# Attention on one Trainium2 core: the 256-column parts of two neighbouring heads share a PSUM bank, one exponential and the last step of the row maximum

## The chip, the cores and the metric

The kernel runs on one core of one Trainium2 chip. The time is device microseconds of that core for one execution of the whole program; lower is better. Instructions are issued to five queues: TensorE (PE: matmuls, and PEld for the weight loads ahead of them), VectorE (DVE), ScalarE (ACT), GpSimd (POOL) and SyncE (SP: DMAs). PSUM has eight banks of 128 x 512 fp32; a tile of scores takes one bank.

## The reference, cut to what matters

Two independent halves are computed and put side by side: attention with a memory that is carried over four segments (`A`), and a two-dimensional spectral filter (`B`, FFT, product, inverse FFT). The change touches the softmax of `A` alone. There are 32 heads of width 18, and each of the 4 segments has 512 rows.

```python
for s in range(N):                      # N = 4 segments of L = 512 rows
    qs, ks, vs = q[:, :, s], k[:, :, s], v[:, :, s]
    logits = jnp.einsum("bhqd,bhkd->bhqk", qs, ks) * scale + mask   # causal
    p = _softmax(logits, axis=-1)
    a_dot = jnp.einsum("bhqk,bhkd->bhqd", p, vs)
    ...                                 # a_mem from M and z, then the gate
    o = g * a_mem + (1.0 - g) * a_dot
outs @ wo
```

## The kernel before, in words

The program has three stages. The FFT and the projections of q, k and v come first, the inverse FFT follows with the first attention steps woven into it, and from about 348 us on there is attention alone, with the output projection and the work on the memory as background. The edits lie in attention.

**Steps and groups.** There are 128 pairs of a head and a segment. The loop in `attention` (L986) has one step `t` for each, and four steps make a group `k` (`k, hh = divmod(t, 4)`; 32 groups). Each step runs two passes over different heads, because the maximum of a row must be known before its exponentials:

- `s1` (L679) makes the scores of pair `t+11`, rows on partitions, to find each row's maximum. The 512 x 512 scores are causal, so the four row blocks have 128, 256, 384 and 512 columns. They go into banks of the pool `ps1` (tag `s1`, three banks) as three tiles, which I call **A** (384 and 128 columns in one bank), **B** (512) and **C** (256). For each block DVE adds the mask and takes the maximum in one instruction (L690), whose result lands in `mg`; the reduced products themselves go to a scratch tile `junk`.
- `mpath` (L698) turns a group's 16 columns of maxima into rows: POOL splits them into two bf16 parts `mh` (L702, L703), PE transposes them into `mt` (L706, which also takes a bank of tag `s1`), ACT copies that to `mts` (L709), and a DMA puts it under `Q` as two more contraction rows. It begins at the end of an even step (`hh==0`) and its transpose stands in the odd step after that (`hh==1`).
- `s2` (L714) makes the scores of pair `t` again, transposed and with the maximum subtracted by those two rows, in three tiles of the pool `ps` (tag `s2`, three banks), **P0** (512 columns, L722), **P1** (384 and 128, L726 and L727) and **P2** (256, L731). ACT turns each into exponentials (L723, L728, L732) in the SBUF tiles `P[0]`, `P[1]`, `P[2]` of the group. When a group's fourth head is done, POOL zeroes what lies above the diagonal (L736, `affine_select`), two tiles at once and two (`rest`) one step later.
- `pv` (L745) is the product with v: in the steps with `t%4==1` and `t%4==3`, a burst of 16 matmul records for the whole group before.

Steps with `hh` 0 or 2 are called even here and have no burst; those with `hh` 1 or 3 are odd and have one. Within a step the order is written out by hand in `attention`: A, P0, B, P1, then the burst in odd steps, then one piece of background (`run_bg`), then C, the transpose where there is one, and P2. PE runs them in this order, and a scheduler does not move them. A tile of `s1` takes the bank of a tile that DVE has finished reading, most often the third one back, so A of a step waits for A of the step before, and so on; where the transpose has taken a bank, the tiles behind it move up by one.

Background that matters below: `combine` (L853), `mem1` (L826) and `oproj` (L891) issue matmuls into the single bank of tag `post`, and DVE multiplies what they make (L836, L881, L883: `am` or `ux` times `pb`). `recip` (L772) puts a reciprocal of 128 x 128 on DVE (L780). From `t=117` on there is no `s1` any more (the tail).

Of the kernel before, what the change touches and what calls it, by code (L numbers as in the profile page):

```python
# [5 lines left out]
F32=mybir.dt.float32; F32R=mybir.dt.float32r  # L6
AF=mybir.ActivationFunctionType; OP=mybir.AluOpType
# [358 lines left out]
BF=mybir.dt.bfloat16  # L366
# [43 lines left out]
class ATT:  # L410
# [268 lines left out]
    def s1(s,t):  # L679

        nc=s.nc; k,hh=divmod(t,4); n,qd=divmod(k,2); h=4*qd+hh
        Q,K=s.Qs[n%3],s.Ks[n%4]; tp=s.sm
        assert (n,0) in s.loaded and (n,1) in s.loaded,(t,n)
        if hh==0: s.mg[k]=tp.tile([128,4,4],F32,name="mg")
        def part(*J):
            p=s.ps1.tile([128,512],F32,name="s1",tag="s1")
            for o,i in J: nc.tensor.matmul(p[:,o:o+128*i+128],Q[:108,h,128*i:128*i+128],K[:108,h,:128*(i+1)],start=True,stop=True)  # L687
            for o,i in J:
                w=128*(i+1); b=256*(1+i//2); junk=tp.tile([128,b],BF,name=f"junk{b}",bufs=1)
                nc.vector.tensor_tensor_reduce(out=junk[:,:w],in0=p[:,o:o+w],in1=s.mask[:,512-w:],scale=1.0,scalar=-3.0e38,  # L690
                    op0=OP.add,op1=OP.max,accum_out=s.mg[k][:,hh,i:i+1])
        part((0,2),(384,0))
        yield
        part((0,3))
        yield
        part((0,1))
        yield
    def mpath(s,k):  # L698

# [14 lines left out]
    def s2(s,t):  # L714
        nc=s.nc; k,hh=divmod(t,4); n,qd=divmod(k,2); h=4*qd+hh
        Q,K=s.Qs[n%3],s.Ks[n%4]; tp=s.tp
        if hh==0: s.P[k]=[tp.tile([128,4,w],F32,name=f"P{i}") for i,w in enumerate((512,512,256))]
        P=s.P[k]
        q=lambda o: Q[:110,h,o:]
        kk=lambda j: K[:110,h,128*j:128*j+128]  # L720
        p0=s.ps.tile([128,512],F32,name="s2",tag="s2")
        nc.tensor.matmul(p0,kk(0),q(0),start=True,stop=True)  # L722
        nc.scalar.activation(P[0][:,hh],p0,AF.Exp,scale=SC)  # L723
        yield
        p1=s.ps.tile([128,512],F32,name="s2",tag="s2")
        nc.tensor.matmul(p1[:,:384],kk(1),q(128),start=True,stop=True)  # L726
        nc.tensor.matmul(p1[:,384:],kk(3),q(384),start=True,stop=True)  # L727
        nc.scalar.activation(P[1][:,hh],p1,AF.Exp,scale=SC)  # L728
        yield
        p2=s.ps.tile([128,256],F32,name="s2",tag="s2")  # L730
        nc.tensor.matmul(p2,kk(2),q(256),start=True,stop=True)  # L731
        nc.scalar.activation(P[2][:,hh],p2,AF.Exp,scale=SC)  # L732
        r=slice(0,4) if k<31 else (slice(0,3) if hh==2 else slice(3,4))
        if hh==3 or k==31 and hh==2:
            def sel(x):
                nc.gpsimd.affine_select(out=x[:,r],in_=x[:,r],pattern=[[0,r.stop-r.start],[1,128]],compare_op=OP.is_ge,fill=0.0,base=0,channel_multiplier=-1)  # L736
            sel(P[0][:,:,:128])
            sel(P[1][:,:,384:])
            def rest():
                sel(P[1][:,:,:128])  # L740
                sel(P[2][:,:,:128])
            if k<31: s.rest=rest
            else: rest()
        yield
    def pv(s,k,jj):  # L745

# [437 lines left out]
```

## Time and profile before

| what | value |
|---|---|
| time, median of 3 executions | 689.67 us (688.49 to 689.87) |
| time of the profiled execution | 689.55 us |
| its span, first to last instruction | 687.8 us |
| PE busy | 671.8 us (98%) |
| DVE busy | 543.0 us (79%) |
| ACT busy | 440.4 us (64%) |
| POOL busy | 192.1 us (28%) |
| granted TensorE clock | 1.00 throughout |
| stretch 618 to 650 us (the tail) | PE busy 29.05 of 32.00 us, DVE 22.85, ACT 22.09 |

Times are from one profiled execution. The 1.75 us between its own time and its span lie outside what the profile shows. The busy time of PE counts each matmul to its modelled end, and such ends overlap the next matmul, so a PE that reads as busy may still be waiting for a bank; waits show as longer distances between the starts of matmuls. In the same way two DVE instructions in a row overlap by some 0.07 us, so a duration is longer than the distance from one start to the next. Rows of the timeline read: start, duration, engine, line, operation, output<-input, size, count, and in square brackets the idle time before and what ended it.

### The profile page before, as it was taken

Reading aid. Unit: us, or ns where it says so; the run is one execution under the profiler, and the core shown is the slowest. Engines: PE = TensorE matmul, PEld = TensorE weight load, DVE = VectorE, ACT = ScalarE, POOL = GpSimd, SP = SyncE. Lnnn points to the kernel's source line nnn. Section 1 sums busy time; section 2 is a strip of 40 time slices with the busy share of each in tenths; the row PEclk is TensorE's granted clock in tenths of the full one; section 3 lists DMA queues with packets and bytes.
Section 4 is the critical chain, followed back from the end, with each engine's and each line's share of the span. In section 5 each row is a group of like instructions: output and inputs, shape, how many; then the busy total and the mean of one; then the engine's idle time right before and its main releaser. Section 6 shows DMA issues by size and latency. Waiting matters only on the chain.

```text
span 687.8 us, 14313 instructions
## 1 busy us (share of the span) xinstructions
PE 671.8 (98%) x4776; PEld 486.7 (71%) x4776; DVE 543.0 (79%) x1509; ACT 440.4 (64%) x964; POOL 192.1 (28%) x389
## 2 busy tenths in 40 slices
PE   9999999999999999999989999999999999998997
PEld 5999779879879879899954444444566445663497
DVE  5998989889789679598678888988856988567643
ACT  3876795675685474544468877777766777666531
POOL 2111000100200102566325533435323563235310
PEclk9999999999999999999999999999999999999999
DMA  9896466595486679799337775765656567423152
GB/s 338 297 307 185 144 190 196 168 302 178 136 235 209 198 207 306 195 282 272 100 107 193 198 185 161 208 191 155 171 154 185 152 171 165 125 80 97 29 166 80
DMA packets 76035, 127.58 MB, mean 185 GB/s; under 512 B 12812, under 2 KB 44202, under 8 KB 72370
## 3 DMA queue, kind: packets, MB, share of 16 engines
q1 hardware_dynamic: 69310, 110.67, 55.7%
q0 software_dynamic: 5632, 15.76, 8.1%
q8 instruction: 37, 0.61, 0.4%
q10 hardware_dynamic: 1020, 0.25, 0.2%
q14 instruction: 36, 0.29, 0.2%
HBM read 81.78 MB, written 43.92 MB: 183 GB/s over the span
## 4 chain that ended last, share of the span: by engine, by line
PE 84%; DVE 5%; ACT 3%; DMA 3%; issue 3%; POOL 1%; SPq 0%; ACTq 0%; DVEq 0%; POOLq 0%
PE pj L487 15%; PE pv L754 11%; PE s L687 11%; PE pjv L487 7%; PE po L902 7%; PE i L331 4%; PE i L320 4%; PE f L145 4%; PE c L166 4%; PE s L722 3%; PE s L726 3%; PE po L931 2%; PE pn L829 2%; DVE junk L690 2%; PE pm L559 2%
## 5 line engine op out<-in xcount | busy, mean ns | idle before, releaser
L690 DVE CUSTOM_DVE_ANT_0 junk<-s,x 128x384 bf16<-128x384 f32 (+3 forms) x512 | 222.7, 487 | 48.1 <-PE s L687 47.2
L736 POOL TENSOR_SCALAR_AFFINE_SELECT P<-P 128x512 f32<-128x512 f32 (+2 forms) x132 | 79.2, 625 | 75.4 <-ACT P L723 73.7
L754 PE MATMUL pv<-P,vs 128*32 128x512 f32 (+3 forms) x1024 | 82.2, 439 | 0.2 <-POOL P L736 0.2
L723 ACT ACTIVATE P<-s 128x512 f32<-128x512 f32 x128 | 77.6, 606 | 6.3 <-PE s L687 2.1
L728 ACT ACTIVATE P<-s 128x512 f32<-128x512 f32 x128 | 77.7, 607 | 3.4 <-PE s L727 3.1
L732 ACT ACTIVATE P<-s 128x256 f32<-128x256 f32 x128 | 49.7, 389 | 45.0 <-PE s L731 44.8
L687 PE MATMUL s<-Ks,Qs 108*128 108x384 bf16 (+3 forms) x256 | 65.2, 300 | 3.0 <-DVE mg L690 2.3
L754 PEld LDWEIGHTS pv<-P,vs 128*32 128x32 f32 x1024 | 26.8, 109 | 45.2 <-issue 34.8
L487 PE MATMUL pj<-x,wqkh 128*128 128x512 f32 x162 | 56.1, 408 | 0.0
L232 DVE TENSOR_TENSOR Z<-Z 128x580 f32<-128x580 f32 (+2 forms) x51 | 45.9, 913 | 0.6
L687 PEld LDWEIGHTS <-Qs 108*128 108x128 bf16 x320 | 31.2, 98 | 19.2 <-issue 12.4
L690 DVE DVE_READ_ACCUMULATOR2_ANT mg<- 128x1 f32 x512 | 42.5, 83 | 0.0
L548 POOL MEMSET vt<- 128x32 f32 x16 | 2.4, 162 | 139.5 <-PE pm L559 125.5
L320 PE MATMUL i<-civ,Y 128*128 128x256 f32 (+1 forms) x288 | 39.7, 290 | 1.0 <-POOL Y L305 0.9
L320 PEld LDWEIGHTS i<-civ,Y 128*128 128x128 f32 (+1 forms) x288 | 36.7, 181 | 2.1 <-POOL Y L305 1.3
L331 PE MATMUL i<-itab,T 128*128 128x290 f32 (+1 forms) x224 | 36.6, 306 | 0.1
L487 PE MATMUL pj<-x,wqkl 128*128 128x512 f32 x90 | 35.6, 395 | 0.0
L487 PE MATMUL pj<-xh,wqkh 128*128 128x512 f32 x90 | 35.5, 395 | 0.0
L487 PE MATMUL pj<-xh,wqkl 128*128 128x512 f32 x90 | 35.5, 395 | 0.0
L487 PEld LDWEIGHTS pj<-x,wqkh 128*128 128x128 f32 x162 | 30.5, 189 | 6.4
L506 DVE SCALAR_TENSOR_TENSOR ex<-pj,ex 128x512 f32<-128x512 f32 (+1 forms) x28 | 19.3, 689 | 19.5 <-ACT ex L504 19.4
L687 PE MATMUL s<-Ks,x 108*128 108x384 bf16 (+3 forms) x128 | 32.7, 299 | 0.6 <-ACT mts L709 0.2
(207 smaller groups left out, 1705.1 us busy)
## 6 DMA issues: line engine op xcount, KB each, us to landing
qkD<-sp SPq DMA_DIRECT2D x32, 384.0 KB
xin<-xb SPq DMA_DIRECT2D x16, 384.0 KB
cfw<-cfw POOLq DMA_DIRECT2D x16, 384.0 KB, 4.8
civ<-civ POOLq DMA_DIRECT2D x16, 384.0 KB, 8.3
Ks<-qkD SPq DMA_DIRECT2D x12, 512.0 KB
x<-qkD SPq DMA_DIRECT2D x10, 512.0 KB
Qs<-qkD SPq DMA_DIRECT2D x10, 512.0 KB
vs<-vD SPq DMA_DIRECT2D x16, 310.5 KB
```

The lines of the kernel that those rows point to most:

```text
L232: s.nc.vector.tensor_tensor(o,a,b,op=op)
L320: nc.tensor.matmul(p[:m,k],Y[i][:,q,c*128:c*128+m],cc[:,hl,o:o+256],start=n==0,stop=n==5)
L331: nc.tensor.matmul(p,x,t,start=n==0,stop=n==6)
L487: s.nc.tensor.matmul(out,a,b,start=i==0,stop=i==len(L)-1)
L687: for o,i in J: nc.tensor.matmul(p[:,o:o+128*i+128],Q[:108,h,128*i:128*i+128],K[:108,h,:128*(i+1)],start=True,stop=True)
L690: nc.vector.tensor_tensor_reduce(out=junk[:,:w],in0=p[:,o:o+w],in1=s.mask[:,512-w:],scale=1.0,scalar=-3.0e38, op0=OP.add,op1=OP.max,accum_ ...
L723: nc.scalar.activation(P[0][:,hh],p0,AF.Exp,scale=SC)
L728: nc.scalar.activation(P[1][:,hh],p1,AF.Exp,scale=SC)
L732: nc.scalar.activation(P[2][:,hh],p2,AF.Exp,scale=SC)
L736: nc.gpsimd.affine_select(out=x[:,r],in_=x[:,r],pattern=[[0,r.stop-r.start],[1,128]],compare_op=OP.is_ge,fill=0.0,base=0,channel_multiplie ...
L754: nc.tensor.matmul(s.pvt[32*hh:32*hh+32,128*j:],vt[:,152*j+19*h:152*j+19*h+32],mv[0][:,hh,mv[1]],start=j==0,stop=j>1,skip_group_check=True)
L902: nc.tensor.matmul(ps,a[t][:r,c],b[:r,t,w],start=i==0,stop=i==13)
```

## The change

The 256-column parts of two neighbouring heads are put into one bank. In `s1` an even head of a group (`hh` 0 or 2 of the first pass) no longer makes a tile C; the odd head makes one tile with both parts, its neighbour's at column 0 and its own at column 256, and DVE reduces the two one after the other. In `s2` an even head no longer makes P2; the odd head makes one 512-column tile with both, and one exponential over 512 columns stands for two over 256. The scratch tiles of the maximum get a third width. The calls of `affine_select` are the same for all groups but the last, where they are split by heads 0 and 1, 2, and 3. `pv` and its place are not touched.

Since the first pass is 11 pairs ahead, its odd heads fall into the even steps: C with two parts stands at the end of even steps, and P2 with two parts at the end of odd steps.

```diff
         def part(*J):
             p=s.ps1.tile([128,512],F32,name="s1",tag="s1")
-            for o,i in J: nc.tensor.matmul(p[:,o:o+128*i+128],Q[:108,h,128*i:128*i+128],K[:108,h,:128*(i+1)],start=True,stop=True)
-            for o,i in J:
-                w=128*(i+1); b=256*(1+i//2); junk=tp.tile([128,b],BF,name=f"junk{b}",bufs=1)
+            for o,i,e in J: nc.tensor.matmul(p[:,o:o+128*i+128],Q[:108,h+e,128*i:128*i+128],K[:108,h+e,:128*(i+1)],start=True,stop=True)
+            for o,i,e in J:
+                w=128*(i+1); b=max(256,w-128*e)
+                junk=tp.tile([128,b],BF,name=f"junk{b}",bufs=1)
                 nc.vector.tensor_tensor_reduce(out=junk[:,:w],in0=p[:,o:o+w],in1=s.mask[:,512-w:],scale=1.0,scalar=-3.0e38,
-                    op0=OP.add,op1=OP.max,accum_out=s.mg[k][:,hh,i:i+1])
-        part((0,2),(384,0))
-        yield
-        part((0,3))
-        yield
-        part((0,1))
+                    op0=OP.add,op1=OP.max,accum_out=s.mg[k][:,hh+e,i:i+1])
+        part((0,2,0),(384,0,0))
+        yield
+        part((0,3,0))
+        yield
+        if hh%2: part((0,1,-1),(256,1,0))
         yield
...
         yield
-        p2=s.ps.tile([128,256],F32,name="s2",tag="s2")
-        nc.tensor.matmul(p2,kk(2),q(256),start=True,stop=True)
-        nc.scalar.activation(P[2][:,hh],p2,AF.Exp,scale=SC)
-        r=slice(0,4) if k<31 else (slice(0,3) if hh==2 else slice(3,4))
...
+        if hh%2:
+            p2=s.ps.tile([128,512],F32,name="s2",tag="s2")
+            for e in (-1,0): nc.tensor.matmul(p2[:,256+256*e:512+256*e],K[:110,h+e,256:384],Q[:110,h+e,256:],start=True,stop=True)
+            nc.scalar.activation(P[2][:,hh-1:hh+1].rearrange("p h c -> p (h c)"),p2,AF.Exp,scale=SC)
...
+        if k==31 and hh>0:
+            a,b=((0,2),(2,3),(3,4))[hh-1]
+            sel(P[0][:,:,:128],a,b)
...
```

The order of the instructions, at a place in the middle of attention (about 375 us of the profile before). First PE from the burst of an odd step to the tile A of the even step behind it, before the change (`mt` is the transpose of the maxima; L687 are scores of the first pass, L731 those of P2):

```order
L754 MATMUL pv<-P_4575,vs 32x512 x4
L754 MATMUL pv<-P_4576,vs 32x128 x4
L687 LDWEIGHTS x_2634
L687 MATMUL s_4777<-Ks_3171,x_2634 128x256
L706 LDWEIGHTS mh
L706 MATMUL mt<-idb,mh 128x128
L731 LDWEIGHTS Ks_3169
L731 MATMUL s_4783<-Qs_3167,Ks_3169 128x256
L687 LDWEIGHTS x_2634
L687 MATMUL s_4790<-Ks_3171,x_2634 128x384
L687 LDWEIGHTS x_2634
L687 MATMUL s_4790<-Ks_3171,x_2634 128x128
```

The same place now (L707 is the transpose, L733 is P2):

```order
L760 MATMUL pv<-P_4554,vs 32x512 x4
L760 MATMUL pv<-P_4555,vs 32x128 x4
L707 LDWEIGHTS mh
L707 MATMUL mt<-idb,mh 128x128
L733 LDWEIGHTS Ks_3169
L733 MATMUL s_4752<-Qs_3167,Ks_3169 128x256
L733 LDWEIGHTS Ks_3169
L733 MATMUL s_4752<-Qs_3167,Ks_3169 128x256
L687 LDWEIGHTS x_2634
L687 MATMUL s_4760<-Ks_3171,x_2634 128x384
L687 LDWEIGHTS x_2634
L687 MATMUL s_4760<-Ks_3171,x_2634 128x128
```

The tile C between burst and transpose is gone, and P2 has two matmuls into one tile; between burst and A stand as many columns as before.

DVE at the same place, from the last reduction of the odd step over the whole even step, before (each ISA row with a `junk` output is a reduction, the row behind it stores its result):

```order
L690 ISA junk_4779,mg<-s_4777,x_2634 128x256
L690 ISA mg 128x1
L690 ISA junk_4793,mg<-s_4790,x_2634 128x384
L690 ISA mg 128x1
L690 ISA junk_4795,mg<-s_4790,x_2634 128x128
L690 ISA mg 128x1
L690 ISA junk_4802,mg<-s_4800,x_2634 128x512
L690 ISA mg 128x1
L690 ISA junk_4811,mg<-s_4809,x_2634 128x256
L690 ISA mg 128x1
L690 ISA junk_4821,mg<-s_4818,x_2634 128x384
```

And now, from the first reduction of the even step to the first of the odd one:

```order
L691 ISA junk_4763,mg<-s_4760,x_2634 128x384
L691 ISA mg 128x1
L691 ISA junk_4765,mg<-s_4760,x_2634 128x128
L691 ISA mg 128x1
L691 ISA junk_4772,mg<-s_4770,x_2634 128x512
L691 ISA mg 128x1
L691 ISA junk_4782,mg<-s_4779,x_2634 128x256
L691 ISA mg 128x1
L691 ISA junk_4784,mg<-s_4779,x_2634 128x256
L691 ISA mg 128x1
L691 ISA junk_4791,mg<-s_4788,x_2634 128x384
```

The reduction of 256 columns that stood ahead of the even step's 384 has moved behind that step's 512: DVE now goes straight from one odd step's 512 to the next even step's 384, and the two reductions of 256 follow each other.

## The prediction on record

> **What bounds the kernel now.** I read the page first, then the groups by line with shapes kept apart, then the timeline of PE and DVE through several pairs of steps, then the waits. Three lines carry the outline:
>
> ```profile
> PE 671.8 (98%) x4776; PEld 486.7 (71%) x4776; DVE 543.0 (79%) x1509; ACT 440.4 (64%) x964; POOL 192.1 (28%) x389
> PE 84%; DVE 5%; ACT 3%; DMA 3%; issue 3%; POOL 1%; SPq 0%; ACTq 0%; DVEq 0%; POOLq 0%
> L732 ACT ACTIVATE P<-s 128x256 f32<-128x256 f32 x128 | 49.7, 389 | 45.0 <-PE s L731 44.8
> L728 ACT ACTIVATE P<-s 128x512 f32<-128x512 f32 x128 | 77.7, 607 | 3.4 <-PE s L727 3.1
> ```
>
> PE is the engine that ends the program; ACT is off the path, and ahead of the very exponentials that the change merges it stands idle for 45 us because PE has not made their scores yet. The change keeps every matmul and its columns, so it can save time only where PE waits. Where that is shows in a plain pair of steps, without background (PE, then DVE):
>
> ```profile
> 443.54 0.28 PE L687 MATMUL s<-Ks,Qs 108*128 108x256 bf16 x1
> 443.77 0.38 PE L687 MATMUL s<-Ks,Qs 108*128 108x384 bf16 x2
> 444.21 0.38 PE L687 MATMUL s<-Ks,Qs 108*128 108x512 bf16 x1
> 444.65 0.27 PE L687 MATMUL s<-Ks,Qs 108*128 108x256 bf16 x1
> 444.76 0.27 PE L731 MATMUL s<-x,Ks 110*128 110x256 bf16 x1
> 445.04 0.38 PE L687 MATMUL s<-Ks,Qs 108*128 108x384 bf16 x2
> 445.67 0.38 PE L687 MATMUL s<-Ks,Qs 108*128 108x512 bf16 x1
> ```
>
> ```profile
> 443.86 0.42 DVE L690 CUSTOM_DVE_ANT_0 junk<-s,x 128x256 bf16<-128x256 f32 x1 [0.45 <-PE s L687]
> 444.21 0.55 DVE L690 CUSTOM_DVE_ANT_0 junk<-s,x 128x384 bf16<-128x384 f32 x1
> 444.92 0.69 DVE L690 CUSTOM_DVE_ANT_0 junk<-s,x 128x512 bf16<-128x512 f32 x1
> 445.53 0.42 DVE L690 CUSTOM_DVE_ANT_0 junk<-s,x 128x256 bf16<-128x256 f32 x1
> 445.88 0.55 DVE L690 CUSTOM_DVE_ANT_0 junk<-s,x 128x384 bf16<-128x384 f32 x1
> ```
>
> Matmuls of 256 columns follow each other at 0.11 us (444.65 to 444.76), and A to B takes 0.44 (443.77 to 444.21). So the odd step's A could start at 444.87; it starts at 445.04, because it needs the bank of the even step's A, whose reductions end as DVE goes on to B at 444.92. Its B could start 0.44 after 444.87, at 445.31, and starts at 445.67, when B's bank is free (DVE goes on at 445.53). PE loses 0.36 us in the pair, all of it to DVE's way through A and B of the even step: 0.71 (444.21 to 444.92) and 0.61 (444.92 to 445.53).
>
> **The change, part by part.**
>
> *Moving C, plain pairs: nothing.* DVE begins the even A at 444.21, 0.44 after PE began it, and that is when the scores are there: C of the odd step, done from 443.86 to 444.21 in what was idle time, ends just then. Without C ahead of it A starts no earlier, B ends no earlier, and the odd step's B still starts at 445.67. PE's columns up to there are the same, two P2 parts in place of C and P2. These pairs keep their 0.36 us.
>
> *Moving C, pairs where DVE is behind: 2.0 us.* In six odd steps DVE waits for the matmul `pb`, multiplies, and only then reduces C. The first and the last of the six (451.85, 461.46, 475.63, 536.85, 546.47, 560.67), and what follows the first on DVE and on PE:
>
> ```profile
> 451.85 0.68 DVE L881 TENSOR_TENSOR am<-ux,pb 72x512 f32<-72x512 f32 x1 [0.57 <-PE pb L878]
> 452.46 0.41 DVE L690 CUSTOM_DVE_ANT_0 junk<-s,x 128x256 bf16<-128x256 f32 x1
> 452.80 0.55 DVE L690 CUSTOM_DVE_ANT_0 junk<-s,x 128x384 bf16<-128x384 f32 x1
> ...
> 560.67 0.69 DVE L836 TENSOR_TENSOR am<-am,pb 126x512 f32<-126x512 f32 x1 [0.71 <-PE pb L835]
> ```
>
> ```profile
> 451.88 0.38 PE L687 MATMUL s<-Ks,Qs 108*128 108x384 bf16 x2
> 453.08 0.27 PE L731 MATMUL s<-x,Ks 110*128 110x256 bf16 x1
> 453.62 0.38 PE L687 MATMUL s<-x,Qs 108*128 108x384 bf16 x2 [0.26 <-DVE mg L690]
> 454.25 0.38 PE L687 MATMUL s<-x,Qs 108*128 108x512 bf16 x1
> ```
>
> The even A was there at 451.88 + 0.44 = 452.32, and DVE came to it at 452.80, 0.34 of that for C (452.46 to 452.80). PE then waits: its next A could have gone at 453.19. With C moved, DVE has done it in the idle time (0.57 and 0.71 in the rows shown) and starts A 0.34 earlier; PE's next A and B follow 0.34 earlier and still wait, so the whole 0.34 counts: 6 x 0.34 = 2.0. From both sides: 0 if a full DVE takes it back one step on; 3.7 if the pair's whole wait goes (its B could start at 453.19 + 0.44 = 453.63 and starts at 454.25: 0.62).
>
> *Fewer tiles in the ring, 0.7 us.* Four times B waited for the bank that the transpose had taken, until ACT had copied `mts`:
>
> ```profile
> PE s L687 <- ACT mts L709: 0.7, 4, 0.2
> 456.54 0.38 PE L687 MATMUL s<-x,Qs 108*128 108x384 bf16 x2
> 457.31 0.38 PE L687 MATMUL s<-x,Qs 108*128 108x512 bf16 x1 [0.17 <-ACT mts L709]
> ```
>
> B could have started 0.44 after A, at 456.98, and lost 0.33. In the changed order the tile that follows three behind the transpose is always C, which comes later than B. Two of the four lie in pairs counted above, so two are added: 0.7 (bounds 0 and 1.3).
>
> *Reciprocals, 0.4 us.* Twice a reciprocal stands between C and the even A, and PE's output projection hides part:
>
> ```profile
> 599.33 0.95 DVE L780 RECIPROCAL ry<-ry 128x128 f32<-128x128 f32 x1
> 600.20 0.49 DVE L690 CUSTOM_DVE_ANT_0 junk<-s,x 128x384 bf16<-128x384 f32 x1
> ...
> 611.86 0.95 DVE L780 RECIPROCAL ry<-ry 128x128 f32<-128x128 f32 x1
> ```
>
> Each gives between 0 and 0.34; I take 0.2, because the projection covers some and I cannot say how much.
>
> *The merged exponential, 0.2 us.* In plain attention nothing waits for it. In the tail ACT is the one that PE waits for:
>
> ```profile
> 636.21 0.38 ACT L732 ACTIVATE P<-s 128x256 f32<-128x256 f32 x1 [1.61 <-PE s L731]
> 636.49 0.59 ACT L723 ACTIVATE P<-s 128x512 f32<-128x512 f32 x1
> 636.97 0.60 ACT L728 ACTIVATE P<-s 128x512 f32<-128x512 f32 x1
> ...
> 636.67 0.27 PE L731 MATMUL s<-x,Ks 110*128 110x256 bf16 x1
> 637.13 0.38 PE L722 MATMUL s<-x,Ks 110*128 110x512 bf16 x1 [0.20 <-ACT P L723]
> 637.62 0.32 PE L726 MATMUL s<-x,Ks 110*128 110x384 bf16 x1
> ```
>
> P0 of the odd step now takes the bank of the merged P2, and P1 that of the even P0. The merged exponential starts 0.11 later (a second matmul) and takes 0.48 to the next start (636.49 to 636.97) in place of 0.28, so the even P0's starts at 636.21 + 0.11 + 0.48 = 636.80 and is done 0.59 later, at 637.39. P1 goes at about 637.44, not 637.62: 0.18, less the 0.11 of the P2 matmul that now comes behind the burst. Three such pairs: 0.2. Bounds: a loss of 0.4, if ACT's background falls in between, and a gain of 1.
>
> *What comes later.* The maxima of a group are complete 0.35 later (one more reduction of 256, 443.86 to 444.21), and behind them are queued POOL's `mh`, the two selects of `rest`, and PE's transpose with P2 behind it:
>
> ```profile
> 446.03 0.20 POOL L702 CAST mh<-mg 128x16 bf16<-128x16 f32 x1 [2.11 <-DVE mg L690]
> 446.31 0.22 POOL L703 TENSOR_TENSOR mh<-mg,mh 128x16 bf16<-128x16 f32 x1
> 447.54 0.22 PE L706 MATMUL mt<-idb,mh 128*128 128x128 bf16 x1
> PE mt L706 <- POOL mh L703: 0.6, 1, 0.6
> ```
>
> `mh` is done at 446.53, the transpose runs at 447.54: 1.0 us of cover, made by the burst, and the only long wait (0.6) was for a busy POOL, which later maxima don't lengthen. I put it at nothing; without that cover it would cost up to 0.35 in each of 32 groups, 11 us. What `rest` makes is used three steps on. Here a rule speaks against the change: the Trainium skill's page "Perfetto Trace Analysis", section "Optimizing Scalar/DVE Operations", advises that where ScalarE and VectorE aren't full but hold up others, their instructions be broken up, so that work completes sooner. By it, both merged pieces would come too late and the sum would turn into the loss of the last rival below; the trace has slack behind both.
>
> The selects of the last group are split into eleven where there were eight, on a POOL that is 28% busy. The third scratch tile costs no instruction.
>
> **Sum:** 2.0 + 0.7 + 0.4 + 0.2 = 3.3 us, against the profiled execution's 689.55 (span 687.8, and 1.75 outside it that stays): 686.2. The median of the runs lies 0.12 above that execution.
>
> **Rivals.**
>
> *The ring was too short everywhere.* A plain pair waits 0.36, and I take half of the 64 pairs to be plain (an estimate). If sending ten tiles of a group through three banks in place of twelve removed that wait, it would be 32 x 0.36 = 11.5 more: 674.7. Against it: in the rows above PE waits until a fixed time after the even A, which DVE needs whatever the number of tiles, and the tile between A and the next A still stands there. I give it 0.08. The Trainium skill says in "Perfetto Trace Analysis", section "Optimization Strategy", that consistent bubbles on the engine that should be full can mean too little PSUM for the next tile; that would be this case, and the trace agrees that there is such a gap, but not that a tile less closes it.
>
> *DVE takes it back.* From 451.85 DVE has hardly a pause for the next steps. If what PE saves there only makes it wait one tile later, the six pairs give nothing, and with the small terms alone (1.3, of which I would then trust half) the time is 688.9. For it: DVE's work in the pair is unchanged. Against it: the pause of 0.57 ahead of it is real idle time, which C now fills. Chance 0.2.
>
> *Two reductions in a row come too late.* The even step now ends with two reductions of 256; the odd step's A and B wait for them on DVE, and the next even step's B needs that B's bank. In the plain pair B of the odd step would be reduced by 445.88 + 0.35 + 0.71 + 0.61 = 447.55, and its bank reopens 0.14 later (445.53 to 445.67), at 447.69. PE wants it at 448.15: the transpose at 447.54, 0.06 for it less the C of 0.11 that stood ahead, 0.22 for P2, 0.44 for A. So there is 0.46 of room. Should the pair of reductions take over 0.46 more than its 0.70, or DVE's background stand in both steps, every further 0.2 costs as much in half of the pairs: 32 x 0.2 = 6.4 us, less the gains of 3.3, 692.6. Against it: reductions of different sizes follow each other without a gap in every row above. Chance 0.12.
>
> **How the numbers follow.** The forecast (between 682.1 and 688.2) has 0.6, the short ring 0.08, a gain taken back 0.2, late reductions 0.12. A measurement of this kernel tells about 0.2% (1.4 us) from no change. Faster by more: 0.6 + 0.08 = 0.68; same 0.2; slower 0.12. The range: low end with the upper bounds of the terms, 3.7 + 1.3 + 0.7 + 1 = 6.7, and 0.7 for the waits of two plain pairs, should they go: 682.1. High end: all gains 0, the tail's loss of 0.4 and a transpose 0.35 late in two groups, 0.7: 690.7. It leaves out the short ring and most of the late reductions, 0.18.
>
> **What would show it.** ACT: 64 exponentials of 512 columns on the line of P2, near 607 ns, none of 256. Plain groups: the transposes still follow each other at the same distance. In the six places DVE goes from the multiplication straight to a 384. The row of PE waiting for `mts` gone. PE's matmul of the transpose not waiting for `mh` more than before. I am wrong if plain groups get shorter (first rival), if the six pairs keep their length (second), or if B of even steps starts later than 0.44 after A (third).

## The result and the profile after

The changed kernel takes 684.0 us, median of 4 runs (683.78 to 684.51), beside 689.77 for the kernel before in the same job: ratio 0.9921, 95% interval 0.9904 to 0.9938. The profiled execution took 683.95, with a span of 682.2. The forecast was 686.2 and faster: right in direction and inside the range, 2.2 us too high.

The page of the changed kernel, busy shares and chain by engine, and the group of the merged exponentials:

```profile
PE 669.0 (98%) x4776; PEld 487.0 (71%) x4776; DVE 541.0 (79%) x1509; ACT 433.5 (64%) x900; POOL 193.0 (28%) x392
PE 84%; DVE 5%; DMA 4%; ACT 3%; issue 2%; POOL 1%; SPq 0%; ACTq 0%; DVEq 0%; POOLq 0%
L734 ACT ACTIVATE P<-s 128x512 f32<-128x512 f32 x64 | 38.3, 598 | 46.3 <-PE s L733 45.4
```

The 128 exponentials of 256 columns have become 64 of 512. ACT has 7 us less to do, and still idles 46 us ahead of them: ACT's saving is not where the time came from. PE is the engine that ends the program, as before.

The same plain pair as in the prediction, PE and then DVE (s1's A, B and double C stand on L687, the double P2 on L733, the transpose on L707):

```profile
441.85 0.39 PE L733 MATMUL s<-Qs,Ks 110*128 110x256 bf16 x2
442.08 0.38 PE L687 MATMUL s<-Ks,Qs 108*128 108x384 bf16 x2
442.52 0.38 PE L687 MATMUL s<-Ks,Qs 108*128 108x512 bf16 x1
443.94 0.38 PE L687 MATMUL s<-Ks,Qs 108*128 108x512 bf16 x1
445.68 0.23 PE L707 MATMUL mt<-idb,mh 128*128 128x128 bf16 x1
```

```profile
442.50 0.56 DVE L691 CUSTOM_DVE_ANT_0 junk<-s,x 128x384 bf16<-128x384 f32 x1 [0.46 <-PE s L687]
443.19 0.69 DVE L691 CUSTOM_DVE_ANT_0 junk<-s,x 128x512 bf16<-128x512 f32 x1
```

B of the even step still starts 0.44 after A (442.08 to 442.52). From the even A to the odd B it was 1.90 (443.77 to 445.67) and is 1.86 (442.08 to 443.94). DVE used to come to A at the moment when C was done, 0.44 after PE began A; now it waits idle for A and begins 0.42 after. Those 0.02 to 0.04 in a pair are the only difference in a plain pair.

The first of the six pairs in which DVE is behind, with the even A of the next pair as the last line:

```profile
450.02 0.68 DVE L887 TENSOR_TENSOR am<-ux,pb 72x512 f32<-72x512 f32 x1 [0.25 <-PE pb L884]
450.62 0.55 DVE L691 CUSTOM_DVE_ANT_0 junk<-s,x 128x384 bf16<-128x384 f32 x1
...
450.04 0.38 PE L687 MATMUL s<-Ks,Qs 108*128 108x384 bf16 x2
452.05 0.38 PE L687 MATMUL s<-x,Qs 108*128 108x512 bf16 x1
454.34 0.38 PE L687 MATMUL s<-x,Qs 108*128 108x384 bf16 x2
```

DVE goes from the multiplication straight to the 384 of A. The odd B comes 2.01 after the even A, where it was 2.37 (451.88 to 454.25), and the pair lasts 4.30, where it was 4.66 (451.88 to 456.54).

Three of the six rows that the view of waits has for PE's matmuls, from the first group of the attention to the last:

```profile
PE s L687 <- DVE mg L691: 2.0, 3, 1.1
PE mt L707 <- DVE mg L691: 0.7, 1, 0.7
...
PE mt L707 <- POOL mh L704: 0.6, 1, 0.6
```

The wait for `mts` (0.7, four times) is gone; the transpose still waits 0.6 for a busy POOL once, and 0.7 for a maximum, once, at the first group.

### The profile page after: what moved, and what is told of

Same layout as the page of the kernel before. It is cut to its first block, busy times and chain, and to the rows that moved or that the text cites. A ratio compares the mean times of both kernels' runs of the same rounds, so it can differ in the third digit from the quotient of the medians.

```text
span 682.2 us, 14101 instructions
## 1 busy us (share of the span) xinstructions
PE 669.0 (98%) x4776; PEld 487.0 (71%) x4776; DVE 541.0 (79%) x1509; ACT 433.5 (64%) x900; POOL 193.0 (28%) x392
## 4 chain that ended last, share of the span: by engine, by line
PE 84%; DVE 5%; DMA 4%; ACT 3%; issue 2%; POOL 1%; SPq 0%; ACTq 0%; DVEq 0%; POOLq 0%
PE pj L487 15%; PE pv L760 11%; PE s L687 11%; PE pjv L487 8%; PE po L908 5%; PE i L331 4%; PE i L320 4%; PE f L145 4%; PE c L166 4%; PE s L723 3%; PE s L727 3%; PE pn L835 2%; PE s L733 2%; PE po L937 2%; PE pm L559 2%
## 5 line engine op out<-in xcount | busy, mean ns | idle before, releaser
L691 DVE CUSTOM_DVE_ANT_0 junk<-s,x 128x384 bf16<-128x384 f32 (+3 forms) x512 | 219.6, 486 | 49.0 <-PE s L687 47.6
L724 ACT ACTIVATE P<-s 128x512 f32<-128x512 f32 x128 | 77.3, 604 | 8.3 <-PE s L723 7.1
L729 ACT ACTIVATE P<-s 128x512 f32<-128x512 f32 x128 | 77.0, 602 | 2.8 <-PE s L728 2.7
L734 ACT ACTIVATE P<-s 128x512 f32<-128x512 f32 x64 | 38.3, 598 | 46.3 <-PE s L733 45.4
L687 PE MATMUL s<-Ks,Qs 108*128 108x512 bf16 (+3 forms) x256 | 57.9, 299 | 2.2 <-DVE mg L691 2.0
L687 PEld LDWEIGHTS <-Qs 108*128 108x128 bf16 x320 | 29.5, 97 | 13.0 <-issue 6.2
L500 ACT CAST sp<-pj 128x512 bf16<-128x512 f32 x36 | 21.3, 591 | 18.1 <-PE pj L487 14.4
```

The source lines that it names most:

```text
L687: for o,i,e in J: nc.tensor.matmul(p[:,o:o+128*i+128],Q[:108,h+e,128*i:128*i+128],K[:108,h+e,:128*(i+1)],start=True,stop=True)
L734: nc.scalar.activation(P[2][:,hh-1:hh+1].rearrange("p h c -> p (h c)"),p2,AF.Exp,scale=SC)
```

## The experiments

The theory at the start was that of the prediction: what pays is that C leaves DVE's way. The rival was that the second ring with its fewer tiles, or the merged exponential, bring as much. Times are medians; each ratio is to runs of the kernel before on the same chip, with a median of 689.2 to 689.5.

### Only the double C, and only the double P2

e1 keeps the new `s1` and takes `s2` as it was; e2 keeps the new `s2` and takes `s1` as it was. Against the changed kernel, at the places that matter:

```diff
# e1_c_only
-        if hh%2:
-            p2=s.ps.tile([128,512],F32,name="s2",tag="s2")
-            for e in (-1,0): nc.tensor.matmul(p2[:,256+256*e:512+256*e],K[:110,h+e,256:384],Q[:110,h+e,256:],start=True,stop=True)
+        p2=s.ps.tile([128,256],F32,name="s2",tag="s2")
+        nc.tensor.matmul(p2,kk(2),q(256),start=True,stop=True)
```

```diff
# e2_p2_only
-        if hh%2: part((0,1,-1),(256,1,0))
+        part((0,1))
```

> Only the double C; P2 stays 256 columns in every step, one exponential each. Theory (C taken out of DVE's way brings the gain): six DVE-bound pairs 2.7 with the mts waits, 0.06 in each of some 20 plain groups, the first groups 0.3; only the tail's 0.2 to 0.4 is missing: 684.3 (683.9 to 685.0), plain groups at 7.73. Rival (the second ring's fewer tiles, or the merged exponential, bring half): 686.5 to 687.5. The 0.8 us that lie ahead of the first attention groups should stand on either side of this by chance, if they are none of the change's: first transpose between 309.9 and 310.9.

> Only the double P2 with its one exponential of 512 columns (and the selects of the last group); C stays in its own step and bank. Theory: the tail's 0.2 and nothing else: 689.5 (689.0 to 690.0), plain groups at 7.79, the six DVE-bound pairs as before. Rival (the merged exponential or the second ring brings half): 686.5 to 687.5.

Measured: e1 683.22, ratio 0.9909 [0.9895, 0.9923]; e2 690.85, ratio 1.0024 [1.0015, 1.0034]. The first theory has the places right and the sizes wrong. That C brings the gain held: in sum the six pairs where DVE is behind last 30.55 us before and 30.56 in e2, 28.48 in e1 and 28.51 after, so their 2.0 is C's alone. But e1 came out 1.1 below its 684.3 and below its range, and e2 1.35 above its 689.5 and above its range: the double P2 alone makes the kernel slower, and the plain groups came to neither the 7.73 nor the 7.79 expected. The rival, that P2 brings half, falls.

A plain group is the four steps from one transpose to the next where no background runs. One plain pair of each, the first matmul behind the burst, the even A and the odd B; and two transposes, between which lies one plain group (before: 439.75 and 447.54; after: 437.95 and 445.68). First e1:

```profile
440.56 0.28 PE L732 MATMUL s<-Qs,Ks 110*128 110x256 bf16 x1
440.68 0.38 PE L687 MATMUL s<-Ks,Qs 108*128 108x384 bf16 x2
442.54 0.38 PE L687 MATMUL s<-Ks,Qs 108*128 108x512 bf16 x1
...
436.78 0.23 PE L707 MATMUL mt<-idb,mh 128*128 128x128 bf16 x1
444.31 0.23 PE L707 MATMUL mt<-idb,mh 128*128 128x128 bf16 x1
```

And e2:

```profile
444.73 0.28 PE L687 MATMUL s<-Ks,Qs 108*128 108x256 bf16 x1
445.07 0.38 PE L687 MATMUL s<-Ks,Qs 108*128 108x384 bf16 x2
446.95 0.38 PE L687 MATMUL s<-Ks,Qs 108*128 108x512 bf16 x1
...
440.82 0.22 PE L706 MATMUL mt<-idb,mh 128*128 128x128 bf16 x1
448.81 0.22 PE L706 MATMUL mt<-idb,mh 128*128 128x128 bf16 x1
```

From the even A to the odd B it takes 1.86 in e1 (440.68 to 442.54) and 1.88 in e2 (445.07 to 446.95), as in both other kernels: that stretch is DVE's. What differs is what PE does between the burst and the even A: one matmul of 256 in e1 (0.12), two before and after the change (0.23), three in e2 (0.34). The plain group follows: 7.53, 7.79 and 7.73, 7.99. Hence a second theory: **every matmul that stands on PE between the burst and the even A is on the path**, since PE will wait a fixed time after that A in any case; taking C from there gains 0.11 in a pair, and putting a second P2 there gives 0.11 back. This is a rule for plain pairs; the six pairs where DVE is behind last as long in e1 as in the changed kernel.

The two parts add up. From the first transpose to the last it is 316.2 us before, 309.2 in e1, 318.6 in e2 and 311.6 in the changed kernel: C gains 7.0 with either form of P2, and the double P2 costs 2.4 to 2.5 with either place of C.

### C ahead of the background

```diff
+            if hh%2: steps(a,1)
             run_bg(s.rate)
             steps(a,1)
```

> The kernel before, with C of the odd steps given out ahead of the step's background (pb and its multiplication, the reciprocals) and no longer behind it; banks, ring, exponentials as before. Theory (C stands in DVE's way between the multiplication and the even A): six pairs 2.0 and the reciprocals 0.2 come, plain groups keep 7.79, the mts waits stay: 687.4 (686.8 to 688.2). Rival (the gain of these pairs comes from one tile less in the ring): 689.7, the six pairs as long as before.

Measured: 687.2, ratio 0.9967 [0.9955, 0.9979]. The sum came as expected, and the places only in part. Its first loaded pair, DVE and then PE:

```profile
451.32 0.42 DVE L690 CUSTOM_DVE_ANT_0 junk<-s,x 128x256 bf16<-128x256 f32 x1 [0.45 <-PE s L687]
451.67 0.68 DVE L881 TENSOR_TENSOR am<-ux,pb 72x512 f32<-72x512 f32 x1
452.27 0.55 DVE L690 CUSTOM_DVE_ANT_0 junk<-s,x 128x384 bf16<-128x384 f32 x1
...
451.45 0.38 PE L687 MATMUL s<-Ks,Qs 108*128 108x384 bf16 x2
455.98 0.38 PE L687 MATMUL s<-x,Qs 108*128 108x384 bf16 x2
```

The pair lasts 4.53, 0.13 less than before and not 0.34, for C's own scores come only just ahead of `pb`, and its reduction pushes the multiplication back in its turn: the changed kernel, whose odd steps have no C at all, gets the whole 0.36. The six pairs together gave 1.0 and not 2.0. Most of the rest came where the output projection runs behind the burst; what makes those pairs shorter was not followed further. So C's place ahead of A does cost time with the banks as they were, which speaks against the rival, but e3 does not show the 0.34; that C is worth it in the changed kernel's order is shown by e1 and e2.

### One more reduction behind the even B

```diff
-        if hh%2: part((0,1,-1),(256,1,0))
+        if hh%2:
+            if t>=11:
+                x=tp.tile([128,256],BF,name="junk256",bufs=1)
+                nc.vector.tensor_tensor_reduce(out=x,in0=s.mask[:,:256],in1=s.mask[:,256:],scale=1.0,scalar=-3.0e38,op0=OP.add,op1=OP.max,accum_out=s.mg[k][:,hh,1:2])
+            part((0,1,-1),(256,1,0))
```

> The changed kernel, with one more reduction of 256 columns (of a constant in SBUF) on DVE ahead of the double C's two, in 59 even steps: three in a row. Theory (there are 0.46 us of room behind the double C in a plain pair): plain groups stay at 7.73, the six or seven pairs in which DVE has no idle time pay 0.35 each: 686.4 (685.5 to 687.5). Rival (no room there: the next B's bank comes too late at once): plain groups 8.0 and more, 692 to 700.

Measured: 689.91, ratio 1.0006 [0.9997, 1.0015]. Two transposes around the plain group that was shown above, and two around a group in which DVE is full; that one's transposes stood at 537.55 and 547.18 in the changed kernel, 9.63 apart:

```profile
442.53 0.56 DVE L700 CUSTOM_DVE_ANT_0 junk<-x 128x256 bf16<-128x256 f32 x1
443.02 0.41 DVE L691 CUSTOM_DVE_ANT_0 junk<-s,x 128x256 bf16<-128x256 f32 x1
...
440.51 0.23 PE L711 MATMUL mt<-idb,mh 128*128 128x128 bf16 x1
448.24 0.23 PE L711 MATMUL mt<-idb,mh 128*128 128x128 bf16 x1
...
541.31 0.23 PE L711 MATMUL mt<-idb,mh 128*128 128x128 bf16 x1
552.30 0.23 PE L711 MATMUL mt<-idb,mh 128*128 128x128 bf16 x1 [0.26 <-DVE mg L691]
```

The added reduction takes 0.49 to the next start, all of the room of 0.46 and a little more, and this plain group stays at 7.73. So do five others of the nine; the remaining three grew by 0.09, 0.09 and 0.25, so the room is just used up. The rival (no room, every plain group longer at once) falls. The loss is 5.9 and not the 2.4 expected, and most of it lies in the groups with background, where this one grew from 9.63 to 10.99 and its transpose had to wait for a maximum. In which of those pairs DVE's lateness decides, and in which that of the maximum, was not taken apart.

### One bank more for s1, one less for s2

Every fourth tile of s1, the transposes counted in, is taken from a pool of one bank of its own.

```diff
-            p=s.ps1.tile([128,512],F32,name="s1",tag="s1")
+            p=s.ring([128,512],F32,"s1")
...
-ps=es.enter_context(PP(tc,"ps",dict(s2=3,pv=1,post=1)))
+ps=es.enter_context(PP(tc,"ps",dict(s2=2,s1x=1,pv=1,post=1)))
```

> The changed kernel with one bank moved from the ring of s2 to that of s1 in the attention: four tiles for the scores whose maxima are taken, two for those that go to the exponential. Theory (in a plain pair PE waits for DVE through the bank three tiles back): with four banks the odd A needs the odd B of the pair before, and the odd B the even A, both long reduced, so the 0.36 of a plain pair goes, plain groups 7.73 - 0.72 = 7.0; what two banks cost on the other ring is not known from any row, an estimate of 0.15 a pair: 675 to 681. Rival (DVE's way through A and B bounds the pair whatever the banks): plain groups stay at 7.7, 683 to 686.

Measured: 696.34, ratio 1.0103 [1.0084, 1.0121]; neither. PE in a plain pair: the even A, P1 of the even step, the odd B:

```profile
375.05 0.38 PE L687 MATMUL s<-Ks,x 108*128 108x384 bf16 x2
375.96 0.32 PE L731 MATMUL s<-Qs,Ks 110*128 110x384 bf16 x1
376.83 0.38 PE L687 MATMUL s<-Ks,x 108*128 108x512 bf16 x1
```

The odd B follows the odd A at once, and the first ring's wait is gone. P1 now comes 0.91 after A, where in the changed kernel it came 0.66 after (442.08 to 442.74): it has to wait until the exponential of the double P2 has left one of two banks. The wait moved from one ring to the other, the plain group became 7.90, and most of the loss lies behind the last transpose (627.61; 68 us from there to the end of the span, against 61 before), where two banks for `s2` also serve the tail.

### The double C ahead of the burst; the double P2 behind the next A

e5 moves the double C, e9 the double P2, e10 both.

```diff
# e5, e10
-            a=s.s1(t+11) if t+11<128 else iter(())
+            a=s.s1(t+10) if t+10<128 else iter(())
...
+            if hh%2: steps(a,1)
             if 4<=t-1<132: s.pv((t-5)//4,(t-5)%4)
# e9, e10
             steps(a,1)
+            if pend: steps(pend,1); pend=None
             steps(b,1)
...
-            steps(b,1)
+            if hh%2 and t<128: pend=b
+            else: steps(b,1)
```

> The changed kernel with the double C ahead of the burst and no longer behind the even B: s1 runs ten pairs ahead and not eleven, so that both heads of a pair of C are there in the odd step, and the path of the maxima goes one or two steps later. Theory: DVE has B and the double C to do while PE runs the burst; the tile three back from the odd A is then the double C of the pair before, and from the odd B the even A, both long reduced: the plain pair loses its 0.36, plain groups 7.0 to 7.1, pairs in which DVE has no idle time gain nothing: 672 to 679. Rival (DVE's work is the bound as it is): 683 to 686.

> The changed kernel with the double P2 given out behind the next even A, no longer between the burst and that A. Theory (what stands on PE between the burst and the even A is on the path, because the odd B waits until a fixed time after that A): each plain pair is shorter by the 0.22 of two matmuls of 256 columns, plain groups 7.73 - 0.44 = 7.3, in all about twice what taking one such matmul away gave (2.4 up to the last transpose): 679 (677.5 to 681). Rival (the double P2's cost lies in its exponential or its bank, not in its place): plain groups 7.7, 683.5 to 684.5.

> Both moves: the double C ahead of the burst and the double P2 behind the next even A. Theory: where no tile waits for DVE any more, the place of P2 is worth nothing in plain pairs: plain groups as with the double C alone ahead of the burst (7.0 to 7.1), and a little gained where DVE is full: 672 to 678, within 1 us of that kernel. Rival (what precedes the even A is on the path still): another 0.44 off each plain group, 668 to 671.

Measured: e5 682.79, ratio 0.9906 [0.9891, 0.992]; e9 780.27, 1.1324 [1.1305, 1.1343]; e10 779.7, 1.1313 [1.1285, 1.1342]. In e5, the even B's reduction and what follows, on DVE and PE:

```profile
381.95 0.69 DVE L691 CUSTOM_DVE_ANT_0 junk<-s,x 128x512 bf16<-128x512 f32 x1
382.56 0.55 DVE L691 CUSTOM_DVE_ANT_0 junk<-s,x 128x384 bf16<-128x384 f32 x1
...
382.70 0.38 PE L687 MATMUL s<-Ks,x 108*128 108x256 bf16 x2
```

The tile that is now three back from the double C is the even B, and C starts 0.14 after DVE is done with it: the wait has moved from the odd A and B to C, and the even A's time still fixes the end of the pair. The best plain groups are 7.70, not 7.0, and the expectation fell; the time lies 0.2 below the rival's 683 to 686.

In e9 and e10 the late P2 of every second group is given out behind the load of later queries, which goes into the same buffer. It waits for that load, and by the order of the program it then reads the later queries in place of its own.

```profile
407.77 0.41 PE L733 MATMUL s<-Qs,Ks 110*128 110x256 bf16 x2 [4.44 <-DMA Qs<-reD]
...
391.98 0.23 PE L707 MATMUL mt<-idb,mh 128*128 128x128 bf16 x1
399.27 0.23 PE L707 MATMUL mt<-idb,mh 128*128 128x128 bf16 x1
```

That is a fault of these two kernels and says nothing on the theories; but the plain groups without a load came out at 7.29 in e9 (391.98 to 399.27) and at 7.36 in e10, which had expected 7.0 to 7.1. Three more kernels followed, in which the step's loads are given out behind the late P2:

```diff
# e12, e13, e14: as e9, and the loads behind P2
-            for _ in range(3 if t%8==0 else 1):
-                if q: q.pop(0)()
-            if qu: qu.pop(0)()
             steps(a,1)
             if pend: steps(pend,1); pend=None
+            for _ in range(3 if t%8==0 else 1):
+                if q: q.pop(0)()
+            if qu: qu.pop(0)()
# e13: the transpose behind A as well;  e14: s2 as before, its odd P2 late
```

> The changed kernel with the double P2 behind the next even A, and now the step's loads given out behind it too, so that no load of the next queries stands between a pair's scores. Theory (what stands on PE between the burst and the even A is on the path): plain groups 7.29, as in the groups without a load of the run before this one; the other groups 0.1 to 0.4 less than in the changed kernel: 678 (676.5 to 680). Rival (P2's place is worth nothing, the groups of 7.29 only caught up after the stalls): plain groups 7.7, 683.5 to 684.5.

> As e12, and the transpose mt of each group behind the even A too, with the double P2 behind it: then nothing stands between the burst and the even A. Theory: one matmul of 128 columns (0.06) less on the path in each group, and a late maximum no longer holds up the even A: plain groups 7.23, 1 to 2 us less than e12: 676.5 (675 to 678). Rival (mt's place is hidden): e12's time.

> The double C alone (P2 of 256 columns with its own exponential in every step), with the odd step's P2 behind the next even A: against e12 only the merging of P2 is undone, nothing stands between burst and even A in either. Theory: plain groups 7.3 as in e12; the tail, where the merged exponential helps, is 1.0 to 1.2 longer: 1.1 above e12, 679.1 (677.5 to 681). Rival (128 exponentials of 256 columns cost ACT time that PE waits for in the attention too): 3 or more above e12.

Measured: e12 677.8, ratio 0.9832 [0.9819, 0.9846]; e13 678.35, 0.9842 [0.9828, 0.9855]; e14 679.27, 0.9856 [0.9843, 0.987]. In e12 nothing is left between the burst and the even A but, once in a group, the transpose:

```profile
437.92 0.39 PE L687 MATMUL s<-Ks,Qs 108*128 108x384 bf16 x2
438.15 0.38 PE L733 MATMUL s<-Qs,Ks 110*128 110x256 bf16 x2
439.79 0.38 PE L687 MATMUL s<-Ks,Qs 108*128 108x512 bf16 x1
...
434.25 0.23 PE L707 MATMUL mt<-idb,mh 128*128 128x128 bf16 x1
441.53 0.23 PE L707 MATMUL mt<-idb,mh 128*128 128x128 bf16 x1
```

From the even A to the odd B it is 1.87 again, the double P2 lies inside that stretch and costs nothing, and the plain group is 7.28, 0.45 less than in the changed kernel (two matmuls of 256 in each of two pairs). The second theory holds, to the size. e12 is the fastest of all, 6.2 us below the changed kernel. e14 has the same plain groups and ends 1.5 later: with P2's place settled, that is what the merged exponential is worth. In the two profiled executions most of it lies behind the last transpose, 59.9 us before the end of the span in e12 and 61.4 in e14, where ACT is waited for; but e14's profiled execution was 1.5 above its median, so the split is rough. The rival (3 or more) falls.

e13 gained nothing, against the theory's 1 to 2 us, and most of its plain groups are 7.35, not 7.23: `mt` stands behind A, A of the odd step needs `mt`'s bank, and ACT copies `mt` only behind the double P2's exponential.

```profile
402.49 0.60 ACT L734 ACTIVATE P<-s 128x512 f32<-128x512 f32 x1 [0.97 <-POOL P L736]
402.98 0.24 ACT L710 COPY mts<-mt 32x128 bf16<-32x128 bf16 x1
...
401.72 0.39 PE L687 MATMUL s<-Ks,Qs 108*128 108x384 bf16 x2
403.49 0.38 PE L723 MATMUL s<-x,Ks 110*128 110x512 bf16 x1
```

The copy ends at 403.22, and the odd step's P0, directly behind its A, is at 403.49, 1.77 after the even A; in e12's group it was 1.53 (402.40 to 403.93).

## Why the prediction was right, and where its sizes were off

**Pairs where DVE is behind: 2.0.** Right, and in its mechanism: the six pairs, from even A to even A, became shorter by 0.36, 0.36, 0.37, 0.25, 0.33 and 0.37, in all 2.0. In the first of them DVE begins A 0.58 after PE began it (450.04 to 450.62), where it was 0.92 (451.88 to 452.80): that is the 0.34 of the sum. e1 and e2 show that C does it and not P2.

**`mts` wait: 0.7, reciprocals: 0.4, tail: 0.2.** The two uncounted pairs with the `mts` wait gave 0.6, the reciprocals' 0.25. From the last transpose to the end of the span it was 60.8 (626.98 to 687.8) and is 60.6 (621.60 to 682.2). PE's wait for ACT there did shrink, from 0.7 in three places to 0.3 in one. That the tail's 0.2 came out to the size is luck: one execution of each kernel can't show so little, for this stretch was 60.2 in e2, 59.9 in e12 and 60.9 in e6 and e13 with the merged exponential, and 60.7 in e3, 61.4 in e14 and 61.8 in e1 without it.

**Plain pairs: nothing.** Here a size was off: 0.03 a pair, since C ended 0.02 to 0.04 behind the moment when A's scores were there and not just then. Groups with little background gave 0.05 to 0.1 each, the first groups 0.3, in all about 1.6 us that the sum does not have. The step weighed "two P2 parts in place of C and P2" rightly, but as one thing: e1 and e2 show two of opposite sign, 0.26 gained in a plain group and 0.20 given back. In the whole time C alone is worth 6.2 us and P2 alone costs 1.4. So the closeness of the forecast is luck in part: from the first transpose to the last the sum had 3.1, and the 4.6 measured are 7.0 from C less 2.4 for P2. Plain groups that get shorter were the prediction's own sign for its first rival; 0.06 a group, where that rival asked for 0.72, is not that rival. The prediction had the gap ahead of the even A in view, found it unchanged, and did not ask what it would be worth to empty it.

**Chance: 0.8.** That much of the 5.6 us between the two spans lies ahead of the attention. The first transpose of all, before, after and in e2:

```profile
310.81 0.23 PE L706 MATMUL mt<-idb,mh 128*128 128x128 bf16 x1
```

```profile
309.99 0.23 PE L707 MATMUL mt<-idb,mh 128*128 128x128 bf16 x1
```

```profile
310.15 0.23 PE L706 MATMUL mt<-idb,mh 128*128 128x128 bf16 x1
```

e2 has the program of before up to there and is 0.66 earlier. Five others (e1, e9, e12, e13, e14), with the program of the changed kernel up to there, have it between 309.49 and 310.89, so 0.82 is within what one execution differs from another. Without it the forecast missed by 1.4 or so, nearly all of it in the plain pairs and in the other groups with little background.

**What comes later: nothing.** Held: the transposes wait as before but for 0.4 at the first group, and e6 put 0.49 more ahead of the maxima without cost in six of nine plain groups.

**The rivals.** The short ring: a bank more does take the wait away (e4), so the wait is one for a bank; the change's fewer tiles did not, as forecast, and the bank had to come from the other ring, which then waited. The Trainium skill's reading of consistent bubbles as too little PSUM ("Perfetto Trace Analysis", section "Optimization Strategy") agrees with the first half of that; the 7.90 of e4 is the other half. DVE taking it back did not happen in the six pairs. Two reductions too late: e6 shows that there was room. By the Trainium skill's advice to break instructions up ("Perfetto Trace Analysis", section "Optimizing Scalar/DVE Operations") the merged pieces would have cost time. P2's merging did cost 1.4 us, yet e12 against e14 shows that it was its place on PE and not its size: behind the next A, the merged form is 1.5 us the faster.

## What to carry to other kernels

Where two engines hand banks back and forth, find the instruction from which the other engine's way is fixed (here the even A, 1.86 to 1.90 us ahead of the odd B in five kernels); what the waiting engine does ahead of it is on the path. What it does behind it, inside the wait, is free as long as it holds up no bank that the next tiles need (P2 in e12 did not, the transpose in e13 did). Work that can stand in either place belongs behind it: 0.45 us a plain group here, and 6.2 us in all, a little more than the 5.8 of the change itself. Whoever puts an instruction behind a later one must take the loads that overwrite its operands along.

## What the runs showed that was not expected

An extra bank doesn't shorten a pair in which another ring has just enough (e4), and another order of the tiles in a ring only names another tile to wait for (e5, e13). In e9, where PE stood idle 4 to 9 us at a time, the mean granted clock was 0.944, against 0.999 in the changed kernel; that the one comes from the other was not tested.
